# Two small reads on ScalarE's queue ahead of the loads of a gated linear attention with an expert layer

## The chip, the core and the metric

The kernel runs on one NeuronCore of a Trainium2 chip. The core has five engines, each with its own in-order instruction stream: TensorE (PE in the profile, with weight loads as PEld), VectorE (DVE), ScalarE (ACT), GpSimd (POOL) and SyncE (SP). DMA transfers are issued by an engine's sequencer, go into that engine's queue, and are moved by 16 DMA engines that the core has. The metric is the device time of one execution in microseconds (us); lower is better.

## What is computed

A gated linear attention over a batch of 4, 8 heads, 768 tokens and 48 values per head, followed by a two-layer network with a leaky ReLU over 3072 tokens of width 384:

```python
f = 1.0 / (1.0 + np.exp(-f_logit))
state = np.zeros((B, H, D, D))
for t in range(S):
    state = f[:, :, t, :, None] * state + np.einsum('bhd,bhe->bhde', k[:, :, t], v[:, :, t])
    y[:, :, t] = np.einsum('bhd,bhde->bhe', q[:, :, t], state)
x = y.transpose(0, 2, 1, 3).reshape(B * S, H * D)
h = x @ w_in                       # 384 -> 2048
out = np.maximum(0.01 * h, h) @ w_out   # 2048 -> 384
```

The inputs q, k, v and f_logit are float32 arrays of shape (4, 8, 768, 48): the 48 values of one token of one head are 192 contiguous bytes, and the tokens of a head follow one another.

## The kernel before

The sequence is cut into 6 chunks of 128 tokens. The work is done in 12 units. Units 0 to 3 are the first two chunks (256 tokens) of one batch each; in them two neighbouring tokens share a partition, so a load moves pieces of 2 x 192 = 384 bytes, and it is split into two halves of four heads (argument a = 0 or 1). Units 4 to 11 are one later chunk of two batches each.

For a unit the kernel loads f, k, q and v; forms the gate's logarithm on ScalarE (gate_e, line 229, and gate_l, line 241); sums it over the tokens with triangular matrices on TensorE (cs, lines 250 to 258); takes exponentials (dec, lines 274 and 275); scales k and q with them on VectorE or GpSimd (line 286); transposes both, multiplies them to scores, masks these, and mixes them with v and the running state. The result xT goes through w_in (up, line 510, and up_pair, line 521), the leaky ReLU on ScalarE (lines 516 and 525) and w_out (down, line 532), is copied to osb (line 543), and stored (line 567).

All inputs are float32 in memory. They land in staging tiles, raw_fk (f and k of a unit) and raw_qv (q and v), six of each. The weights are loaded through the last two of each kind and cast to bf16.

The order of everything is written out by hand, as a list of words in a string; each engine takes its own in that order. A word such as `Lk_0_1` is the load of k for unit 0, heads 4 to 7. All loads and stores are issued by SyncE; `load` (lines 159 to 170) could use ScalarE's queue, but no word in the list asks for it. The list begins:

```
c0 Lf_0_1 Lf_0_0 zs_1_0 Lk_0_1 ge_0_1 zk_2 zk_1 zv_1_0 gl_0_1 ge_0_0 zs_2_1 Lq_0_1 Lf_1_0 Lk_0_0 Lf_1_1 ...
```

So SyncE's issues are, in order: f (unit 0, heads 4 to 7), f (unit 0, heads 0 to 3), k and q (unit 0, heads 4 to 7), f (unit 1), k (unit 0, heads 0 to 3), f (unit 1), and on. The first weight load, `WI_2`, is the nineteenth. ScalarE's stream begins with the load of its table of functions (line 56). TensorE runs products of a constant tile, whose results nothing uses, in the gaps of the start (`F_18` and others, line 135).

The program gives its DMAs eight completion counters in turn, and an issue waits for the landing of the DMA that had the same counter before it.

Of the kernel before, what the change touches and what calls it, by code (L numbers as in the profile page):

```python
# [9 lines left out]
FP32 = mybir.dt.float32  # L10
# [5 lines left out]
def kernel(  # L16
# [10 lines left out]
    nc = tc.nc  # L27

    B, H, S, D = q.shape
    assert (B, H, S, D) == (4, 8, 768, 48)  # L30
    C = 128
# [20 lines left out]
    const = ctx.enter_context(tc.tile_pool(name="const", bufs=1))  # L52
    psum = ctx.enter_context(tc.tile_pool(name="psum", bufs=1, space=bass.MemoryType.PSUM))
    ctx.enter_context(tc.manual_schedule())

    nc.scalar.preload_act_table_set("natural_log_exp_and_others")

# [623 lines left out]
```

## Time and profile before

| | us |
|---|---|
| median of 3 timed runs | 176.87 (176.82 to 177.32) |
| the profiled execution | 177.9 |
| its span, first to last instruction | 175.9 |
| TensorE busy | 167.3 |
| ScalarE busy | 107.5 |
| VectorE busy | 83.5 |
| GpSimd busy | 64.8 |
| granted TensorE clock | 0.999 |

The profile is one execution. Its page gives busy times, the span in 40 slices of 4.4 us with a digit for the busy tenth of each, the DMA queues, and the chain of work that ended last. A row of the timeline reads: start in us, length in us, engine, line, operation, output<-input, shapes, and in brackets the idle time of the engine just before with what ended it. A row of the chain of waits reads: start, length, what; SPq is SyncE's sequencer issuing a DMA. A row of the DMA issues ends with the KB of one and the median us from issue to landing. HBM reads of 25.17 MB and writes of 4.72 MB make 170 GB/s over the span.

### The profile page before, as it was taken

How to read it: one execution, taken by the hardware profiler on the slowest of the kernel's cores; microseconds unless marked ns; L12 is line 12 of the kernel's file. 1: busy time of each engine (PE TensorE's matmuls, PEld its weight loads, DVE VectorE, ACT ScalarE, POOL GpSimd, SP SyncE). 2: the span in 40 equal slices, each digit the busy share in tenths (PEclk: the TensorE clock that was granted, in tenths of full speed). 3: DMA queues.
4: the chain of work that ended last, by engine and by line, in shares of the span. 5: the costliest groups of instructions: out<-in, count | busy, mean ns of one | idle time of the engine just before them, and what ended most of it. 6: DMA issues, size and time to landing. Idle time of an engine off the chain costs nothing.

```text
span 175.9 us, 5142 instructions
## 1 busy us (share of the span) xinstructions
PE 167.3 (95%) x2095; PEld 105.0 (60%) x2095; DVE 83.5 (47%) x169; ACT 107.5 (61%) x233; POOL 64.8 (37%) x149
## 2 busy tenths in 40 slices
PE   7788989999999999999999999999999999999993
PEld 2555678797666785744565754565734555645662
DVE  4488787555138407602465770838622308510010
ACT  4775497797753681499960489900599930477411
POOL 7558686353401972200266565001462222000000
PEclk9999999999999999999999999999999999999999
DMA  5999999999999889897999999999989994132004
GB/s 125 279 296 312 317 292 364 364 306 247 241 198 198 149 175 197 159 200 150 197 240 139 248 217 218 177 147 188 267 174 213 173 200 126 46 137 93 0 22 157
DMA packets 110535, 34.93 MB, mean 199 GB/s; under 512 B 102960, under 2 KB 109744, under 8 KB 110512
## 3 DMA queue, kind: packets, MB, share of 16 engines
q1 hardware_dynamic: 110512, 34.61, 85.2%
q8 instruction: 16, 0.26, 0.6%
q14 instruction: 7, 0.06, 0.1%
HBM read 25.17 MB, written 4.72 MB: 170 GB/s over the span
## 4 chain that ended last, share of the span: by engine, by line
PE 63%; DMA 13%; SPq 11%; issue 4%; POOL 3%; DVE 3%; ACT 1%; POOLq 0%; DVEq 0%
PE ps L532 24%; PE ps L521 19%; PE ps L510 9%; SPq L164 6%; DMA out_dram<-osb 6%; SPq L168 5%; DMA raw_fk<-in_moe_w_in_dram 4%; PE ps L393 3%; DMA kT<-kh 3%; PE ps L548 2%; PE ps L362 1%; DVE wm L376 1%; POOL kh L286 1%; PE ps L258 1%; PE ps L463 1%
## 5 line engine op out<-in xcount | busy, mean ns | idle before, releaser
L532 PE MATMUL ps<-w_out,gT 128*128 128x384 bf16 x368 | 65.8, 326 | 0.0
L532 PEld LDWEIGHTS <-gT 128*128 128x128 bf16 x368 | 34.3, 98 | 22.5
L521 PE MATMUL ps<-xT,w_in 128*128 128x512 bf16 x192 | 44.4, 379 | 0.5 <-DVE osb L543 0.5
L525 ACT ACTIVATE gT<-ps 128x512 bf16<-128x512 f32 x64 | 35.1, 631 | 6.1 <-PE ps L521 6.0
L521 PEld LDWEIGHTS <-w_in 128*128 128x128 bf16 x192 | 18.4, 98 | 21.4 <-issue 1.3
L376 DVE TENSOR_TENSOR wm<-ps,ut 128x512 bf16<-128x512 f32 x32 | 19.9, 683 | 15.8 <-PE ps L362 6.2
L291 POOL CAST vb<-raw_qv 128x384 bf16<-128x384 f32 (+1 forms) x16 | 10.6, 664 | 37.0 <-DMA raw_qv<-in_v_dram 36.8
L510 PE MATMUL ps<-xT,w_in 128*128 128x256 bf16 x192 | 23.3, 273 | 0.8 <-ACT xT L445 0.5
L543 DVE COPY osb<-ps 128x384 f32<-128x384 f32 x14 | 7.6, 554 | 31.9 <-PE ps L532 19.2
L516 ACT ACTIVATE gT<-ps 128x512 bf16<-128x512 f32 x32 | 17.6, 624 | 5.7 <-PE ps L510 5.5
L510 PEld LDWEIGHTS <-w_in 128*128 128x128 bf16 x192 | 18.2, 98 | 3.9 <-ACT w_in L200 0.5
L229 ACT ACTIVATE e<-raw_fk 128x384 f32<-128x384 f32 (+1 forms) x16 | 10.9, 689 | 15.1 <-DMA raw_fk<-in_f_logit_dram 14.9
L274 ACT ACTIVATE em<-ps 128x384 bf16<-128x384 f32 x24 | 12.2, 508 | 11.5 <-PE ps L261 10.0
L445 ACT CAST xT<-ps 128x384 bf16<-128x384 f32 x14 | 6.7, 502 | 16.8 <-PE ps L393 16.6
L483 POOL CAST sb<-sf 64x192 bf16<-64x192 f32 x40 | 13.7, 343 | 8.2 <-DVE sf L473 6.0
L480 POOL TENSOR_TENSOR sf<-sf,end 128x192 f32<-128x192 f32 x16 | 8.1, 505 | 19.0 <-DVE sf L475 18.6
L286 DVE TENSOR_TENSOR kh<-raw_fk,em 128x384 bf16<-128x384 f32 (+1 forms) x10 | 8.7, 866 | 13.5 <-DMA raw_fk<-in_k_dram 7.1
L475 DVE TENSOR_TENSOR sf<-sf,ps 64x192 f32<-64x192 f32 x32 | 11.2, 350 | 5.1 <-PE ps L463 2.2
L286 DVE TENSOR_TENSOR qh<-raw_qv,at 128x384 bf16<-128x384 f32 (+1 forms) x12 | 9.3, 789 | 8.3 <-ACT at L275 7.8
L275 ACT ACTIVATE at<-ps 128x384 bf16<-128x384 f32 x24 | 12.4, 515 | 0.0
L286 POOL TENSOR_TENSOR kh<-raw_fk,em 128x384 bf16<-128x384 f32 (+1 forms) x6 | 8.5, 1410 | 8.1 <-ACT em L274 3.6
L241 ACT ACTIVATE lf<-e 128x384 bf16<-128x384 f32 (+1 forms) x16 | 10.9, 684 | 0.3
(92 smaller groups left out, 182.5 us busy)
## 6 DMA issues: line engine op xcount, KB each, us to landing
out_dram<-osb SPq DMA_DIRECT2D x23, 192.0 KB, 3.2
raw_fk<-in_f_logit_dram SPq DMA_DIRECT2D x22, 192.0 KB, 4.0
raw_fk<-in_k_dram SPq DMA_DIRECT2D x22, 192.0 KB, 4.0
raw_qv<-in_q_dram SPq DMA_DIRECT2D x22, 192.0 KB, 4.0
raw_qv<-in_v_dram SPq DMA_DIRECT2D x22, 192.0 KB, 4.0
raw_fk<-in_moe_w_out_dram SPq DMA_DIRECT2D x2, 768.0 KB, 8.4
raw_qv<-in_moe_w_out_dram SPq DMA_DIRECT2D x2, 768.0 KB, 7.3
raw_fk<-in_moe_w_in_dram SPq DMA_DIRECT2D x1, 768.0 KB, 6.7
```

Source lines behind the costliest of these rows:

```text
L229: nc.scalar.activation(e[:, part], src[:, part], AF.Exp, scale=-1.0)
L274: nc.scalar.activation(ems[j % 2][:, a], t[:, 0:H * D], AF.Exp, scale=1.0)
L275: nc.scalar.activation(ats[j % 2][:, a], t[:, 0:H * D], AF.Exp, scale=-1.0)
L286: eng.tensor_mul(heads(j, to[j % NR], a)[:, :, :, 0:D], raw_heads(j, x, a), decays(j, by, a))
L376: nc.vector.tensor_mul(w, src.rearrange("t (p n) -> t p n", p=P2), ut[:, None, :].to_broadcast([128, P2, 128]))
L475: nc.vector.tensor_add(sf[rows], sf[rows], new)
L483: nc.gpsimd.tensor_copy(out=sb[rows, :, y * D:y * D + D], in_=sf[rows])
L510: nc.tensor.matmul(pm[:, i, :], w_in_of(ff, kk), xTs[j // 2 % 2][:, kk, j % 2].rearrange("t a s -> t (a s)"), start=(kk == 0), stop=(kk == ...
L516: nc.scalar.activation(dst, pm, AF.Prelu, alpha=0.01)
L521: nc.tensor.matmul(banks[bank], w_in_of(ff, kk), xTs[j // 2 % 2][:, kk].rearrange("t u a s -> t (u a s)"), start=(kk == 0), stop=(kk == NK ...
L525: nc.scalar.activation(g_blocks(j)[ff], banks[st[j].pop(("pm", ff))], AF.Prelu, alpha=0.01)
L532: nc.tensor.matmul(po, g_of(j, ff, a), w_out_b[quarter][:, ff % 4, :], start=(ff == 0), stop=(ff == NF - 1))
```

## The change

Before anything else on ScalarE, two DMAs are issued on ScalarE's own queue. For k and then for q, each reads the first of the 48 values for every sixteenth token of unit 0's 256 tokens and each of the 8 heads: 16 x 8 single words of 4 bytes, with tokens 16 x 192 = 3072 bytes apart within a head. They land in a new tile of 16 partitions, which no later instruction reads. The rest of the program is as it was.

```diff
@@ -52,6 +52,10 @@
     const = ctx.enter_context(tc.tile_pool(name="const", bufs=1))
     psum = ctx.enter_context(tc.tile_pool(name="psum", bufs=1, space=bass.MemoryType.PSUM))
     ctx.enter_context(tc.manual_schedule())
+
+    first_words = const.tile([16, 2, H], FP32, tag="first_words")
+    for i, t in enumerate((k, q)):
+        nc.scalar.dma_start(out=first_words[:, i], in_=t[0, :, 0:2 * C:16, 0].rearrange("h t -> t h"))
 
     nc.scalar.preload_act_table_set("natural_log_exp_and_others")
 
```

## The prediction

> **What bounds the kernel now.** I read the page's busy times and slices first, for what is full and when, then the chain that ended last, for what the start waits for, and then the first 20 us closely, since the change stands at the program's first instruction.
>
> ```profile
> PE 167.3 (95%) x2095; PEld 105.0 (60%) x2095; DVE 83.5 (47%) x169; ACT 107.5 (61%) x233; POOL 64.8 (37%) x149
> DMA  5999999999999889897999999999989994132004
> q1 hardware_dynamic: 110512, 34.61, 85.2%
> ...
> PE 63%; DMA 13%; SPq 11%; issue 4%; POOL 3%; DVE 3%; ACT 1%; POOLq 0%; DVEq 0%
> ```
>
> TensorE is busy 95%, but part of that is the filler of line 135. The DMA row stands at 9 from the second slice on: after 4.4 us the 16 engines stream without a pause. One queue, q1, moves everything; ScalarE issues no DMA today. The chain in order of time gives the start:
>
> ```profile
> 0.74 0.45 SPq L164
> ...
> 3.98 1.38 SPq L164
> ...
> 12.52 6.74 DMA raw_fk<-in_moe_w_in_dram
> ...
> 19.28 0.63 ACT w_in L200
> ...
> 19.95 2.31 PE ps L510 x18
> ```
>
> From 0.74 to 12.52 the chain is SyncE issuing loads one behind another. Then comes the first weight load (6.74 us), its cast on ScalarE, and at 19.95 the first real up-projection. So until 20 us the bound is the stream of loads in its issue order. One issue stands out: at 3.98 the seventh load takes 1.38 us where the ones ahead took 0.5, because the queue ahead of it moved slowly. That stretch, cut into windows (columns: window, length, busy us of PE, PEld, DVE, ACT, POOL, granted clock, DMA share, GB/s):
>
> ```profile
> 2.50:3.50 1.00, 1.00 (x4) 0.30 (x2) 0.32 (x3) 0.00 (x0) 0.85 (x7) 1.00 1.08 296
> 3.50:5.50 2.00, 2.00 (x13) 0.98 (x12) 0.00 (x0) 1.93 (x5) 2.00 (x8) 1.00 0.93 208
> 5.50:7.50 2.00, 1.34 (x17) 0.95 (x16) 1.35 (x3) 1.18 (x5) 1.37 (x6) 1.00 1.14 309
> 8.50:10.50 2.00, 1.58 (x33) 1.17 (x32) 1.32 (x3) 1.97 (x7) 0.12 (x1) 1.00 1.08 285
> 1.50:2.50 1.00, 1.00 (x4) 0.41 (x3) 1.00 (x8) 0.51 (x1) 0.82 (x5) 1.00 0.43 95
> ```
>
> The stream runs at 296 GB/s before and 309 after, but at 208 from 3.5 to 5.5. Three loads of 192 KB take 0.59 MB, so the first two (f, f) pass until about 3.5 to 4.1, and the slow stretch holds the third and fourth: the first reads of k and of q. When the loads landed, by the issues before 3 us (last column: us from issue to landing; the 2.8 is the median of the three f loads):
>
> ```profile
> raw_fk<-in_f_logit_dram SPq DMA_DIRECT2D x3, 192.0 KB, 2.8
> raw_fk<-in_k_dram SPq DMA_DIRECT2D x1, 192.0 KB, 4.2
> raw_qv<-in_q_dram SPq DMA_DIRECT2D x1, 192.0 KB, 4.3
> ```
>
> ```profile
> 1.25 0.49 SPq L164
> ...
> 1.78 0.50 SPq L164
> ...
> 2.33 0.51 SPq L164
> ```
>
> The second f load, issued at 1.25, lands at about 4.05; k, issued at 1.78, at 5.98; q, issued at 2.33, at 6.63. At 300 GB/s a load of 192 KB (197 kB) needs 0.66 us. The step from f to k is 1.93 us, so 1.3 us too long; the step to q is 0.65, as it should be. Who waits for these loads:
>
> ```profile
> 0.73 1.28 ACT L56 ACT_TABLE_LOAD   x1 [0.73 <-PEq L665]
> 3.51 0.52 ACT L229 ACTIVATE e<-raw_fk 128x384 f32<-128x384 f32 x1 [1.50 <-DMA raw_fk<-in_f_logit_dram]
> 5.47 0.49 ACT L274 ACTIVATE em<-ps 128x384 bf16<-128x384 f32 x1
> 6.07 0.56 DVE L286 TENSOR_TENSOR kh<-raw_fk,em 128x384 bf16<-128x384 f32 x1 [3.25 <-DMA raw_fk<-in_k_dram]
> 7.24 0.52 ACT L229 ACTIVATE e<-raw_fk 128x384 f32<-128x384 f32 x1 [0.82 <-DMA raw_fk<-in_f_logit_dram]
> 13.62 0.52 ACT L229 ACTIVATE e<-raw_fk 128x384 f32<-128x384 f32 x1 [1.37 <-DMA raw_fk<-in_f_logit_dram]
> 16.48 0.91 POOL L286 TENSOR_TENSOR qh<-raw_qv,at 128x384 bf16<-128x384 f32 x1 [0.72 <-DMA raw_qv<-in_q_dram]
> 19.28 0.62 ACT L200 CAST w_in<-raw_fk 128x512 bf16<-128x512 f32 x1 [0.51 <-DMA raw_fk<-in_moe_w_in_dram]
> ```
>
> ScalarE, VectorE and GpSimd come to rest on a load again and again (1.50, 3.25, 0.82, 1.37, 0.72, 0.51 us). If the stream were earlier, they would be too.
>
> **The change, part by part.** Nothing is removed. Two DMA issues go ahead of the table load on ScalarE. Each moves 128 single words, 16 tokens by 8 heads, into 16 partitions; nothing reads them.
>
> *The issues on ScalarE.* No issue on this engine is in the trace. SyncE's nearest rows are 0.45 to 0.51 us, so two cost about 1.0 us. The table load would run from 1.73 to 3.01 instead of 0.73 to 2.01. The first instruction behind it waits for f until 3.51, and 1.50 us of that wait is idle: the 1.0 us is hidden, with 0.5 us left. Each microsecond beyond 1.5 would delay the first Exp by as much; at twice SyncE's price that is 0.5 us. I take nothing, bounds 0 and +0.5.
>
> *The words themselves.* 256 packets over 16 engines are 16 each. The mean packet of q1 takes 85.2% of 175.9 us times 16 engines over 110512, which is 21.7 ns, so 16 of them cost 0.35 us in the stream as an upper end. The lower end is nothing, where they run before the first f packets (the window from 1.5 has a DMA share of 0.43 only). They are far smaller than that mean packet, so I take +0.2.
>
> The Trainium skill says in DMA: Bandwidth & Descriptors, "Issuing engines are not separate DMA queues", that DMAs issued by different engines run on the same 16 DMA engines and interleave. By that rule none of the words is free and the term is the full +0.35 rather than +0.2; no row here has a second queue to show it.
>
> *What they may save.* If the slow stretch is the price of touching k and q for the first time, paid by each DMA engine, the words pay it from about 1.85 us on, beside f, and the real loads find it paid. The mean over the engines is (300 - 208)/300 of 2.0 us, 0.61 us. By the landing of k it is 1.3 us, since a load has landed only with its slowest engine. What lands at 19.26 is set by a slow engine again, perhaps another one. I take the middle, -0.95, with bounds 0 and -1.3.
>
> *The sum* is -0.95 + 0.2 + 0 = -0.75 us at the first weight load, now landing 12.52 + 6.74 = 19.26. It carries on: behind it come the cast, then TensorE at 19.95, and the queue behind this load holds the rest of the stream. What I see of the end of that:
>
> ```profile
> 43.61 8.45 PE ps L532 x52
> ...
> 74.23 5.51 DMA out_dram<-osb
> ...
> 130.38 5.99 PE ps L521 x27
> ```
>
> To 54 us the chain is TensorE, back to back, then links of issue and landing that each start from the one before, then TensorE again. No link starts at a fixed time, so I let nearly all of it through: -0.7. The profiled execution has a span of 175.9 us and 2.0 us around it (177.9 in all), 1.0 above the median of 176.87, so 177.2 in a profiled run, and **176.2 us** in the timed ones. A measurement here tells about 0.3% (0.53 us) from no change; this is 0.4%.
>
> *Waits that are added.* The program counts landings on eight counters in turn, and an issue waits for the DMA eight earlier. Two counters now go to the words first, so SyncE's seventh and eighth issues (3.98 and 5.39) wait for the words to land. If a word takes the whole 1.3 us beyond 1.85, they land by 3.2: no wait. Were they later, the third f load and all behind it would be late, but five loads stand queued ahead, some 3 us of stream. The new tile also moves all later tiles by its 64 bytes a partition; no cost is taken.
>
> **The rivals.**
>
> *The gain is hidden.* The stream gets earlier but another engine lags on w_in, or the compute chain ends as late as now. For it: em is ready at 5.96 (5.47 + 0.49), only 0.11 ahead of kh. Against it: the later waits for loads, up to 1.37 us. Net -0.2: 176.7.
>
> *The stretch is no first touch.* Then the words save nothing and cost 0.2 to 0.35: 177.1. For it: the first reads of v, issued from 6.54 on, land in 3.8 us like their neighbours, and the window they fall into has 285 GB/s:
>
> ```profile
> raw_qv<-in_v_dram SPq DMA_DIRECT2D x3, 192.0 KB, 3.8
> ```
>
> Against it: the stretch falls on the first k and q, and f's first microsecond is slow too (95 GB/s from 1.5 to 2.5, ramp included).
>
> The HBM Reference of the Trainium skill, "Latency", gives 0.2 us on average and 2 us at high load. By that rule it is load that makes a read slow, not a first touch, and the sum would be this rival's. The trace does not settle it: the stretch has less traffic than the windows about it.
>
> *Paid twice; the other side.* The words stand 16 tokens of 192 bytes apart, 3 KB. If what has to be touched is smaller, or is dropped again before the real load comes, the words stall every engine once more, in front of f, and k and q stall as now. The price is 0.61 for the second stall and 0.2 for the words: +0.8, 177.7. It decides where f lands: now 3.51, then above 4.1. Then kh starts at 6.07 + 0.6 or later, and the whole stream behind f with it. For it: v shows that not every first touch costs, so the cause may be finer than a tensor. Against it: the second k load of the same unit, and those of unit one, show no such stretch (309 GB/s from 5.5).
>
> **How the numbers follow.** The forecast has 0.46 (own range 175.5 to 176.5), hidden 0.08, no first touch 0.14, paid twice 0.32. Faster by over 0.3% (below 176.34) is the forecast but for 0.02: 0.44. Within are that 0.02, the hidden gain, 0.12 of no first touch and 0.03 of paid twice: 0.25. Slower is the rest, 0.29 and 0.02: 0.31. The range is 175.4 (gain 1.3 with free words is 175.6, a little below for the carry) to 177.8 (paid twice at the full 0.35).
>
> **What would show it.** Right: ScalarE's issues done by 1.8 and the first Exp still at about 3.5; 3.5 to 5.5 at some 300 GB/s; the seventh issue back at 0.55; kh held by em, not k; the first weight load landing near 18.5. Wrong: f landing above 4 (paid twice); 208 GB/s as now with f on time (no first touch); weights early but the last store as now (hidden). An Exp behind a late table load would break the issue term.

## The result, and the profile after

The changed kernel is slower: the ratio of its time to that of the kernel before is 1.0079 (95% interval 1.0054 to 1.0105), or some 1.4 us of 177. The plain medians of 22 runs each, 178.40 and 177.77 us, lie only 0.63 us apart; why they lie closer than the ratio says is not on record, but the same kernel measured again (below) gives 1.0104. The profiled execution took 178.59 us with a span of 176.6 (before: 177.9 and 175.9).

ScalarE's timeline of the changed kernel (start and length in us, engine, line, operation; its lines are four higher than before, so the first Exp is line 233). ACTq is ScalarE's sequencer issuing a DMA:

```profile
0.73 0.43 ACTq L58 DMA_DIRECT2D first_words<-in_k_dram  x1
1.20 0.45 ACTq L58 DMA_DIRECT2D first_words<-in_q_dram  x1
1.68 1.28 ACT L60 ACT_TABLE_LOAD   x1 [1.68 <-PEq L669]
3.63 0.52 ACT L233 ACTIVATE e<-raw_fk 128x384 f32<-128x384 f32 x1 [0.66 <-DMA raw_fk<-in_f_logit_dram]
```

The issues do what was forecast: they push the table load back by 0.95 us, and the wait for f hides it, with 0.66 us left. The first Exp starts 0.12 us later than before. The DMAs issued before 3 us, with the median us to landing:

```profile
raw_fk<-in_f_logit_dram SPq DMA_DIRECT2D x3, 192.0 KB, 3.1
raw_fk<-in_k_dram SPq DMA_DIRECT2D x1, 192.0 KB, 4.7
raw_qv<-in_q_dram SPq DMA_DIRECT2D x1, 192.0 KB, 4.8
first_words<-in_k_dram ACTq DMA_DIRECT2D x1, 0.5 KB, 2.2
first_words<-in_q_dram ACTq DMA_DIRECT2D x1, 0.5 KB, 2.6
```

The words have landed by 2.9 and 3.8 us, ahead of k, and k still takes 4.7 us (4.2 before). The same windows as in the prediction:

```profile
2.50:3.50 1.00, 1.00 (x4) 0.30 (x2) 0.32 (x3) 0.47 (x1) 0.85 (x7) 1.00 1.12 287
3.50:5.50 2.00, 2.00 (x9) 1.06 (x8) 0.00 (x0) 1.81 (x4) 2.00 (x9) 1.00 0.99 235
5.50:7.50 2.00, 1.43 (x21) 1.00 (x18) 0.81 (x2) 1.12 (x4) 1.00 (x6) 1.00 1.07 269
8.50:10.50 2.00, 1.49 (x25) 1.25 (x25) 0.78 (x2) 1.97 (x6) 0.00 (x0) 0.58 1.10 252
```

The slow stretch from 3.5 to 5.5 us is still there, at 235 GB/s. What is new stands behind it: 269 and 252 GB/s where the kernel before had 309 and 285, although the DMA share is as high as before. The stream of loads has become slower as such. The chain of waits shows what it costs:

```profile
3.99 1.67 SPq L168
...
13.49 7.22 DMA raw_fk<-in_moe_w_in_dram
20.71 0.02 issue
20.74 0.63 ACT w_in L204
...
21.41 2.31 PE ps L514 x18
```

The first weight load lands at 20.71 instead of 19.26 us. To see why, here is the DMA summary of the 5 us from 8 to 13 in both kernels, a stretch in which all data moves in 384-byte pieces (some 3% of the packets are single words of 4 bytes; columns of q1: packets, MB, time that the packets took as a share of 16 engines). Before:

```profile
DMA packets 3893, 1.45 MB, mean 290 GB/s; under 512 B 3893, under 2 KB 3893, under 8 KB 3893
q1 hardware_dynamic: 3893, 1.45, 108.5%
```

After:

```profile
DMA packets 3494, 1.30 MB, mean 260 GB/s; under 512 B 3494, under 2 KB 3494, under 8 KB 3494
q1 hardware_dynamic: 3494, 1.30, 109.9%
```

One packet took 1.085 x 16 x 5 us / 3893 = 22.3 ns before and 25.2 ns after. The pieces are the same size and come in the same order. What differs for them is where in the partition they land: the new tile of 64 bytes was allocated first, and everything behind it, the staging tiles included, moved by 64 bytes. That gave theory A, the shift, against theory B, the reads.

### The profile page after: what moved, and what is told of

Read it like the earlier page. It is cut to its first block, busy times and chain, and to the rows that moved or that the text cites. A ratio compares the mean times of both kernels' runs of the same rounds, so it can differ in the third digit from the quotient of the medians.

```text
span 176.6 us, 5144 instructions
## 1 busy us (share of the span) xinstructions
PE 168.2 (95%) x2095; PEld 106.4 (60%) x2095; DVE 83.1 (47%) x169; ACT 108.0 (61%) x233; POOL 64.2 (36%) x149
## 4 chain that ended last, share of the span: by engine, by line
PE 82%; SPq 7%; DMA 6%; ACT 1%; issue 1%; POOL 1%; DVE 0%; POOLq 0%
PE ps L536 32%; PE ps L525 24%; PE ps L514 12%; SPq L168 7%; PE ps L397 5%; DMA raw_fk<-in_moe_w_in_dram 4%; PE ps L366 2%; DMA raw_qv<-in_v_dram 2%; PE ps L552 2%; PE ps L262 1%; PE ps L467 1%; PE ps L359 1%; PE ps L323 1%; PE ps L462 1%; PE ps L265 0%
## 5 line engine op out<-in xcount | busy, mean ns | idle before, releaser
L290 DVE TENSOR_TENSOR kh<-raw_fk,em 128x384 bf16<-128x384 f32 (+1 forms) x10 | 7.8, 781 | 16.1 <-ACT em L278 5.0
L290 POOL TENSOR_TENSOR kh<-raw_fk,em 128x384 bf16<-128x384 f32 (+1 forms) x6 | 8.0, 1328 | 9.2 <-ACT em L278 3.6
```

The costliest lines, as they stand in the source:

```text
L290: eng.tensor_mul(heads(j, to[j % NR], a)[:, :, :, 0:D], raw_heads(j, x, a), decays(j, by, a))
```

## The experiments: shift or reads

**The tile alone.** Against the kernel before:

```diff
+    first_words = const.tile([16, 2, H], FP32, tag="first_words")
```

> The new 64-byte tile is allocated ahead of all others and stays empty; the two reads are left out. So every later tile stands 64 bytes further on in its partition, as in the changed kernel (raw_fk0 at byte 16576 instead of 16512: 192 instead of 128 past a multiple of 256), and nothing else differs from before. Theory A (the shift of the tiles makes the loads of 384-byte pieces dearer; from the profile after: a mean of 24 to 26 ns for such a packet from 5.5 us on, instead of 22.5 to 22.8): as slow as the changed kernel, ratio about 1.008, and the first weight load lands at about 20.5 instead of 19.3 us. Theory B (the reads themselves delay the stream): ratio 1.000, landing at about 19.3.

Ratio 1.0089 (1.0057 to 1.0120). An empty tile, never written or read, costs all that the change costs. From 8 to 13 us:

```profile
DMA packets 3511, 1.31 MB, mean 262 GB/s; under 512 B 3511, under 2 KB 3511, under 8 KB 3511
q1 hardware_dynamic: 3511, 1.31, 127.8%
```

That is 1.278 x 80 / 3511 = 29.1 ns a packet, and 262 GB/s.

**The reads with their tile behind all others.** Against the changed kernel, the tile and the reads stand just behind the last allocation; ScalarE's order is the same:

```diff
-    first_words = const.tile([16, 2, H], FP32, tag="first_words")
-    for i, t in enumerate((k, q)):
-        nc.scalar.dma_start(out=first_words[:, i], in_=t[0, :, 0:2 * C:16, 0].rearrange("h t -> t h"))
...
-    nc.scalar.preload_act_table_set("natural_log_exp_and_others")
...
     w_out_b = tiles(NW, [128, 4, KD], BF16, "w_out")
+    first_words = const.tile([16, 2, H], FP32, tag="first_words")
+    for i, t in enumerate((k, q)):
+        nc.scalar.dma_start(out=first_words[:, i], in_=t[0, :, 0:2 * C:16, 0].rearrange("h t -> t h"))
+    nc.scalar.preload_act_table_set("natural_log_exp_and_others")
```

> Both reads are issued as in the changed kernel, but their tile is allocated behind all others, so every other tile stands where it stood before. Theory A (shift): ratio 1.000 to 1.002, the 384-byte packets from 5.5 us on back at a mean of 22.5 to 22.8 ns, and the first weight load at about 19.5 us. Theory B (reads): ratio about 1.008, the landing at about 20.5 us.

Ratio 1.0019 (0.9984 to 1.0054), and the packets are back:

```profile
DMA packets 3961, 1.48 MB, mean 295 GB/s; under 512 B 3961, under 2 KB 3961, under 8 KB 3961
q1 hardware_dynamic: 3961, 1.48, 111.1%
```

**The reads with a tile of 256 bytes.**

```diff
-    first_words = const.tile([16, 2, H], FP32, tag="first_words")
+    first_words = const.tile([16, 8, H], FP32, tag="first_words")
```

> The changed kernel with the tile widened from 64 to 256 bytes a partition, so that all later tiles move by 256 bytes and keep their place within a block of 256 bytes (raw_fk0 at 16768, 128 past a multiple of 256, as before). Theory A in the form that the place within 256 bytes counts: ratio 1.000 to 1.002. Theory B (reads): about 1.008. If the tile-last kernel is at 1.000 and this one at 1.008, it is another block size or the order of the tiles that counts.

Ratio 1.0005 (0.9978 to 1.0033). From 8 to 13 us:

```profile
DMA packets 3998, 1.49 MB, mean 298 GB/s; under 512 B 3998, under 2 KB 3998, under 8 KB 3998
```

So it is not the order of the tiles, nor any move, but the place within a grid.

**The changed kernel again.**

> The changed kernel once more, on the chip and in the rounds of the other three, for a second profile. Every theory expects a ratio of about 1.008. If its profile has the slow stretch of the first k and q again and the wider steps of about 0.70 us from load to load behind it, both belong to the kernel; if the steps are 0.60 us, they belonged to one execution.

Ratio 1.0104 (1.0050 to 1.0159). The slow stretch is there again (244 GB/s from 3.5 to 5.5 us), and so is the slower stream, at 261 GB/s and 29.0 ns a packet:

```profile
DMA packets 3507, 1.31 MB, mean 261 GB/s; under 512 B 3507, under 2 KB 3507, under 8 KB 3507
q1 hardware_dynamic: 3507, 1.31, 127.0%
```

## The experiments: which grid, and which tiles

These four have no reads. Each adds an empty tile to the kernel before, ahead of the staging tiles or behind them, or (the third) one in each place. In the cut below, b stands for a number of bytes:

```diff
     ctx.enter_context(tc.manual_schedule())
+    ahead = const.tile([16, b // 4], FP32, tag="ahead")
...
     raw_qv = tiles(NB, [128, 2, 2, H, D], FP32, "raw_qv")
+    behind = const.tile([16, b // 4], FP32, tag="behind")
```

**128 bytes ahead.**

> Before with an empty tile of 128 bytes ahead of all others and no reads: raw_fk0 at 0 past a multiple of 256 instead of 128. The pieces of 384 bytes then start at 0 and 128 past a multiple of 256 in turn, as before. Theory A1 (a piece is dear when its start is off the multiples of 128, so that it touches a third block of 256 bytes or ends off a boundary): ratio 1.000, packets at 22.5 ns, steps of 0.60 us from load to load. Theory A2 (any move away from the tuned addresses costs): about 1.008.

Ratio 1.0027 (0.9993 to 1.0062). From 8 to 13 us:

```profile
DMA packets 3939, 1.47 MB, mean 293 GB/s; under 512 B 3939, under 2 KB 3939, under 8 KB 3939
```

A move by 128 bytes leaves the stream as it was.

**32 bytes ahead.**

> Before with an empty tile of 32 bytes ahead of all others and no reads: raw_fk0 160 past a multiple of 256. The pieces start at 160 and 32. Theory A1: they are off the multiples of 128 as with 64 bytes, so ratio about 1.008 and packets at 27 to 30 ns; if starts off the multiples of 64 cost more again, above 1.008. Theory A2: about 1.008 as well, so this run tells the size of the grid, not A1 from A2. If only a move by 64 exactly hurts: 1.000.

Ratio 1.0121 (1.0083 to 1.0158):

```profile
DMA packets 3510, 1.31 MB, mean 261 GB/s; under 512 B 3510, under 2 KB 3510, under 8 KB 3510
q1 hardware_dynamic: 3510, 1.31, 122.2%
```

Off by 32 bytes, the rate is the same 261 GB/s as off by 64; the intervals of the ratios overlap, so they do not tell whether the kernel loses more. This kernel also shows something that the move by 64 does not: its 192-byte packets, those of the later units' loads, have become longer. Mean durations of all 65536 such packets in each trace:

```
before            15.7 ns
64 bytes, no read 15.5 ns
32 bytes          17.4 ns
```

**64 bytes ahead of the staging tiles, 192 behind them.**

> Before with an empty tile of 64 bytes ahead of the twelve staging tiles raw_fk and raw_qv and one of 192 bytes behind them, no reads: only the targets of the loads move by 64 bytes, all other tiles by 256. Theory A1, where the loads carry it: ratio about 1.008, packets of 384 bytes at a mean of 29 to 30 ns from 8 us on. Rival (the engines' own tiles, the transposes' targets or the stores' sources carry it): 1.000, packets at 22.5 ns.

Ratio 1.0107 (1.0056 to 1.0157):

```profile
DMA packets 3510, 1.31 MB, mean 261 GB/s; under 512 B 3510, under 2 KB 3510, under 8 KB 3510
q1 hardware_dynamic: 3510, 1.31, 127.8%
```

**64 bytes just behind the staging tiles.**

> Before with an empty tile of 64 bytes just behind the staging tiles, no reads: the staging tiles stay, everything else moves by 64 bytes. Theory A1, where the loads carry it: ratio 1.000, packets at 22.5 ns. Rival (the other tiles carry it): about 1.008.

Ratio 1.0027 (0.9992 to 1.0061):

```profile
DMA packets 4069, 1.52 MB, mean 303 GB/s; under 512 B 4069, under 2 KB 4069, under 8 KB 4069
q1 hardware_dynamic: 4069, 1.52, 112.4%
```

The staging tiles carry it alone. It is the loads into them that suffer and not the engines' reading out of them: in the kernel with only the staging moved, ScalarE's first six Exps from raw_fk take 522 ns on average, as before. All the other tiles (the engines' tiles, the transposes' targets, the sources of the stores) can be moved by 64 bytes without a loss that shows beside it. The ten profiles so far together; the last column is the start of ScalarE's cast of the first weight load, or of whichever engine's cast came first:

| kernel | first staging tile, bytes past a multiple of 256 | ratio | GB/s, 8 to 13 us | first cast, us |
|---|---|---|---|---|
| before | 128 | 1 | 290 | 19.28 |
| reads, tile last | 128 | 1.0019 | 295 | 18.75 |
| reads, 256-byte tile | 128 | 1.0005 | 298 | 18.03 |
| 128 bytes ahead | 0 | 1.0027 | 293 | 18.41 |
| 64 bytes behind the staging | 128 | 1.0027 | 303 | 18.73 |
| changed kernel | 192 | 1.0079 | 260 | 20.74 |
| changed kernel again | 192 | 1.0104 | 261 | 20.08 |
| tile alone | 192 | 1.0089 | 262 | 19.35 |
| staging moved alone | 192 | 1.0107 | 261 | 19.57 |
| 32 bytes ahead | 160 | 1.0121 | 261 | 20.16 |

The two groups are far apart in rate, with or without the reads, and do not overlap in the first cast (though 19.28 and 19.35 nearly meet): 18.64 us on average at 0 or 128, 19.98 at 160 or 192. The 1.34 us between them is 0.8% of 177 us, so it covers what the whole kernel loses at the least (0.8%) and leaves some 0.8 us of the largest loss (1.2%) without a place. It also follows from the rates. Of the 18 loads ahead of the first weight load the last 14 come after the slow stretch, 14 x 0.197 MB = 2.75 MB; at 296 GB/s (the mean of the first group) they take 9.3 us, at 261 they take 10.5.

## The experiments: what the slow stretch is not

The stretch from 3.5 to 5.5 us, on which the prediction built its gain, stands in all ten profiles, at 208 to 260 GB/s (in the five with the slower stream, at 235 to 258, it is hardly below their later 261). The 208 of the kernel before is the deepest of them, and its long seventh issue (1.38 us) is no mark of a first touch either. Two kernels without the reads, 128 bytes ahead and 64 bytes behind the staging, touch k and q for the first time in the same third and fourth loads, and their seventh issue takes 0.60 and 0.73 us:

```profile
4.00 0.60 SPq L166 DMA_DIRECT2D raw_fk<-in_f_logit_dram  x1
...
4.00 0.73 SPq L165 DMA_DIRECT2D raw_fk<-in_f_logit_dram  x1
```

In both, kh then waits for em and not for k, and the first cast comes at 18.41 and 18.73 us. So three of the signs that the prediction named for a gain (a short seventh issue, kh held by em, the first weights near 18.5 us) come out without any reads: a part of what it took for the price of a first touch was the chance of one execution.

Two further kernels ask whether the stretch belongs to the first touch of k and q.

**Both f loads of unit 1 ahead of the first k and q.**

```diff
-    c0 Lf_0_1 Lf_0_0 zs_1_0 Lk_0_1 ge_0_1 zk_2 zk_1 zv_1_0 gl_0_1 ge_0_0 zs_2_1 Lq_0_1 Lf_1_0 Lk_0_0 Lf_1_1 zv_0_1
+    c0 Lf_0_1 Lf_0_0 zs_1_0 Lf_1_0 ge_0_1 zk_2 zk_1 zv_1_0 gl_0_1 ge_0_0 zs_2_1 Lf_1_1 Lk_0_1 Lq_0_1 Lk_0_0 zv_0_1
```

> Before with SyncE's order at the start changed: both f loads of unit 1 go ahead of the first k and q, so k comes fifth and q sixth (k third, q fourth before). First touch of k and q as the cause of the slow stretch: the window from 3.5 to 5.0 us, now with f in it, runs at about 300 GB/s, and the slow stretch moves with k to about 5.0 to 6.5 us. Rival (the stretch belongs to that time of the start, whatever is loaded): 3.5 to 5.5 us stays at 200 to 260 GB/s, and 5.5 to 6.5 is at about 310. On the time: kh of unit 0 waits some 1.2 us longer for k, so no faster than before.

```profile
3.50:5.50 2.00, 2.00 (x13) 1.01 (x12) 0.00 (x0) 1.88 (x4) 2.00 (x8) 1.00 1.01 250
5.50:7.50 2.00, 0.88 (x12) 0.61 (x10) 0.60 (x2) 1.95 (x6) 1.01 (x6) 1.00 1.08 286
```

Ratio 1.0022 (0.9974 to 1.0071). With f in the stretch it runs at 250 GB/s all the same, and with k and q in the window behind it that one is at 286, a little under the 301 to 309 of the five profiles with the old rate. But from 5.0 to 6.5 us, where the stretch would be if it had moved with k, the half microseconds run at 289, 297 and 320 GB/s.

**The first k and q loads read f.**

```diff
-                                  in_=srcs[x][j, h, 0:2 * C, :].rearrange("h (t s) d -> t h (s d)", s=2))
+                                  in_=srcs["f" if x in "kq" and (j, a) == (0, 1) else x][j, h, 0:2 * C, :].rearrange("h (t s) d -> t h (s d)", s=2))
```

> Before, but the first load of k and the first load of q (unit 0, heads 4 to 7) read the rows of f_logit that the first load has just read, so that half of unit 0 is computed from f in place of k and q. Same pieces, same targets, same order, no first touch of k or q before the sixth load. First touch as the cause: 3.5 to 5.5 us at about 300 GB/s, and the stretch shows up later, at the first true k (from about 5.5 us on). Rival (time of the start): 200 to 260 GB/s from 3.5 to 5.5 us, as in the profiles so far.

```profile
3.50:5.50 2.00, 1.89 (x15) 0.99 (x14) 0.00 (x0) 1.94 (x5) 2.00 (x9) 1.00 0.97 252
5.50:7.50 2.00, 1.47 (x17) 0.99 (x17) 1.58 (x4) 1.40 (x5) 1.67 (x6) 1.00 1.08 296
```

One execution, 176.22 us; it computes half of unit 0 from f in place of k and q. Rows that had been read a microsecond before give the same stretch, 252 GB/s. It belongs to that time of the start, or to the third load in the queue, and not to k and q, as far as one profile of each kernel can tell. What makes it was not tried further and stays open.

## Why the prediction was wrong, step by step

- **What bounds the start** (the stream of loads up to the first weight load): right. A stream with 12% less rate was enough to slow the kernel, and the lost time shows where the prediction looked for the gain, at the first weight load.
- **"What they may save", -0.95 us**: wrong. I had taken a slow stretch with k and q in it for the price of a first touch of k and q. With the words landed before k, the stretch remained (229 and 260 GB/s at the old places; 208, 230 and 250 without the reads); with f in the place of k, it remained. The term is nothing: both kernels that have the reads and the old places within 256 bytes measure within 0.2% of before. The rival for this, with v as its evidence, had been given 0.14.
- **"The words themselves", +0.2, and the issues on ScalarE, 0**: right in size. The issues took 0.43 and 0.45 us instead of the 0.5 assumed, the first Exp moved by 0.12 us, and in the whole time nothing can be told from zero (1.0019 and 1.0005, intervals with 1 in them). Their packets ran from 1.78 to 3.19 us, beside those of f (from 1.86 on) and not ahead of them; whether they cost +0.2 or +0.35 the runs cannot tell.
- **The added waits, 0**: right. The words for q landed later than worked out, at 3.8 us and not by 3.2. But the seventh issue, which has the counter of the words for k (landed at 2.9), started at 3.99 as before (3.98), and the eighth, which has that of q, only at 5.70.
- **"The new tile also moves all later tiles by its 64 bytes a partition; no cost is taken"**: this is the step that failed. It is the whole result: the tile alone gives 1.0089, and 262 GB/s in place of 290 to 303. No number stood behind the "no cost".
- **The rival "paid twice"** came nearest in time (177.7 us, +0.8 where +1.4 was measured), but not by its mechanism: f was to land above 4.1 us and reached ScalarE at 3.63.

In DMA: Bandwidth & Descriptors, "How a descriptor splits into AXI transactions", the Trainium skill says that a descriptor is split at multiples of 256 bytes into transactions, counted in beats of 32 bytes, and that one which does not start at such a multiple also pays for the bytes from the multiple below its start. It tells this of bytes that are fetched; to count so for the targets of the loads, one descriptor to a piece, is my step, and what comes of it is an estimate: a piece of 384 bytes that starts at 0 or 128 has 12 or 16 beats, at 64 or 192 it has 14 or 18, so 16 in place of 14 on average, +14%. The measured time per byte rose by 296/261, +13%, so for the move by 64 the traces agree. For the move by 32 the count gives 15 beats, +7%, and the traces do not agree: 261 GB/s again, so the measurement decides, and the count is not shown to be the cause. Pieces of 192 bytes have the same four starting places with and without a move by 64, and their packets stayed at 15.5 to 15.7 ns; with a move by 32 the count gives 40 beats for four in place of 36, +11%, and the packets went from 15.7 to 17.4 ns, +11%; but this is a length of packets, which is no sure measure of a rate (see the last paragraph). Shown is that the place of the targets sets the rate; by what mechanism stays open.

## What to carry to other kernels

A small tile that is allocated ahead of others is a change to every address behind it: allocate new tiles last, or in multiples of 256 bytes, and compare with a kernel that has the tile alone. Where a stream of DMAs in small pieces bounds a stage, the place of its targets within 128 bytes is worth 12% of its rate here (0 against 32 and 64 was tried, with pieces of 384 bytes). A slow stretch in a trace belongs to what is loaded in it only once something else has been loaded there, and its depth in one execution is not yet a price.

## What the runs showed that I had not expected

The granted clock of TensorE fell in some executions where the loads came late. The tile alone, from 10.5 to 13.5 us (the column before the DMA share):

```profile
10.50:13.50 3.00, 2.64 (x31) 1.78 (x31) 2.67 (x6) 1.78 (x6) 1.91 (x6) 0.53 1.28 261
```

The changed kernel's first profile shows 0.58 from 8.5 to 10.5 us, while the kernel with only the staging moved has the same 261 GB/s with the clock at 1.00:

```profile
10.50:13.50 3.00, 2.80 (x52) 1.92 (x53) 2.54 (x6) 1.38 (x4) 2.27 (x7) 1.00 1.28 261
```

So the slower stream does not come from the clock. The clock may be a part of the lost time: of the timed runs whose mean clock is on record, it was below 0.998 in 24 of 51 of the kernels with the slower stream and in 20 of 123 of the others; where in the run it fell is not on record. It is not all of it. In runs at 0.998 or more, the tile alone took 178.32 us on average (3 runs) and the kernel before, on the same chip, 176.92 (19); the 32 bytes 178.26 (6) and before 176.47 (22). What a lower clock adds where it falls was not measured by itself.

The length of a packet in the trace is no measure of a queue's rate by itself: the changed kernel's first profile had 25.2 ns a packet, the second 29.0, at 260 and 261 GB/s.
